# A planned retention-and-MLP kernel: scaled values issued behind their masks, a smaller lead of attention, and a new order of the first loads

## The chip, the cores and the metric

The kernel runs on one core of one Trainium2 chip. The metric is the device time of one execution in microseconds (us). Shares and durations come from one profiled execution of the kernel before; its instructions are named by their line in the kernel, as L442. PE is TensorE (matmuls), PEld its weight loads, DVE is VectorE, ACT is ScalarE, POOL is GpSimd and SP is SyncE. POOL issues the loads of this kernel; SP issues its stores and the DMA transposes.

## What is computed

Retention (attention with a decay in place of a softmax) over 8 batches, 8 heads, 576 positions and 64 dimensions a head, and behind it an MLP with an exact GELU on the 4608 tokens:

```python
scores = scale * np.matmul(q, k.transpose(0, 1, 3, 2))
Dmat = np.where(rel >= 0, gamma[:, None, None] ** rel[None, :, :], 0.0)
attn = np.matmul(scores * Dmat[None], v)                 # 8 x 8 x 576 x 64
x = attn.transpose(0, 2, 1, 3).reshape(4608, 512)
h = x @ w_in                                             # 512 -> 2048
g = 0.5 * h * (1.0 + erf(h / sqrt(2)))
out = g @ w_out                                          # 2048 -> 512, float32
```

All inputs are float32 in memory. The kernel turns them to bf16 in the loading DMA.

## The kernel before

**Units.** The work of attention is cut into 36 units of 128 tokens. Units 0 to 3 are the first 128 positions of batches 0 to 3. Then come, for each pair of batches, two units for each further 128 positions (4 and 5, 6 and 7, 8 and 9 for the first pair) and one unit that holds the last 64 positions of both batches (10 for the first pair; 11 and 12 are positions 128 to 255 of the second pair, 17 is its tail, and so on). A unit whose positions are the first 128 of its batch is called raw: it uses v as it is loaded. For every other unit v is first multiplied by a decay on DVE, `scaled_v`, L334 to L341, which writes the tile vh.

**Steps of a unit.** T: q and k are turned, for units 0 to 7 on PE (`turn`, L285, tile qk_ps, copied to qkT), from unit 8 on by a DMA transpose that SP issues (`turn_dma`, L298). A: 8 matmuls make the scores (`scores`, L307), and two DVE multiplications mask them (`masked`, L318, tile ret). B: 8 matmuls with v or vh (`inner`, L343, tile o_ps). U: the running state of a pair of batches takes in k and vh (`state`, L360, tile u_ps). X: 4 matmuls with that state (`cross`, L393), and one multiplication or copy that writes the unit's 128 columns of xT (`evacuate`, L407).

**Blocks.** The MLP runs in 9 blocks of 512 tokens, that is of 4 units: `mlp1` (L437) multiplies xT by w_in, 64 matmuls of 512 columns a block, with a GELU on ACT; `mlp2` (L460) multiplies by w_out, 64 matmuls a block, then ACT copies and SP stores. Blocks 0 and 1 have their mlp1 cut into two halves of 256 tokens (L496), so that it can begin with two units; from block 2 on it needs all four units of its block.

**Who sets the order.** The file is a planner. While it writes the program it keeps a model of the time of each engine (`T`), of the landing of each load (`sw_dma`, L169) and of each DMA transpose (`turn_dma`), and at each step it issues what its model says is ready. Only the order of instructions on each engine comes from it. On the chip each engine takes its instructions in that order and waits at each for its inputs, whatever the model thought.

**Loads.** POOL issues them in the order of a list written out by hand, `ORDER` (L223): `q1` is q of unit 1, `wi3` the fourth eighth of w_in, `wo0` the first eighth of w_out, `io` the constants on POOL, `dq2` a POOL multiplication for a decay table. When a pair's state has taken in its k and vh, the loads of a later unit (11 and up) are put behind the list (`reload`, L389). q and k of unit 0 come by two DMAs of SP and ACT (L97).

**Lead of attention.** In blocks before the last, step A is allowed in places between the matmuls of mlp2, and only while the number of units begun is at most four times the block's number plus `AHEAD` (L616). Together with A of a group (a pair, or a tail) the planner issues B and X of the groups before it, when their masks are done.

**When v is scaled.** `fire` (L535) issues `scaled_v` for units in a fixed order as soon as the model says that v has landed (L551 to L556), up to six units before the states that use them.

**Warm-up.** Six matmuls on zeros (L570) run before the first data; in later gaps before 16 us of planned time the planner fills with more of them (L673).

Of the kernel before, what the change touches and what calls it, by code (L numbers as in the profile page):

```python
# [17 lines left out]
def kernel(  # L18
# [24 lines left out]
    N_DF = d_ff // 128  # L43
# [18 lines left out]
    kept = pair_of[1, 0]  # L62
# [6 lines left out]
    N_LD = 9  # L69
    N_QKT = 8  # L70
    N_VH = 6
    AHEAD = 11

    const = ctx.enter_context(tc.tile_pool(name="const", bufs=1))
    ld_pool = ctx.enter_context(tc.tile_pool(name="ld", bufs=N_LD))
# [84 lines left out]


    sw = [0.0]
    flying = []
    dq_done = {1}
    land = {}
# [3 lines left out]
    def sw_dma(issue, move):  # L169
        if len(flying) >= 8:  # L170
            T["pool"] = max(T["pool"], flying[-8])
        at = T["pool"]
        T["pool"] += issue
        sw[0] = max(sw[0] + move, at + 4.95 + move - 0.9)
        flying.append(sw[0])
        return sw[0]

# [7 lines left out]
    def load(what, i):  # L185
# [30 lines left out]
        else:  # L216
# [3 lines left out]
    tiles_of(0)  # L220
    land["q", 0], land["k", 0] = 4.5, 4.6
    cast_due = {("q", 0): (loaded[0][0][:, 0], first["q32"]), ("k", 0): (loaded[0][0][:, 1], first["k32"])}
    ORDER = ("q1 k1 wi0 io v1 q2 k2 q3 k3 v0 v3 wi1 v2 wi2 k4 wi3 wi4 wi5 wi6 q4 v4 wo0 k5 wi7 q5 wo1 wo2 wo3 v5 k6 q6 "  # L223
             "wo4 q7 v8 k7 dq2 wo5 wo6 q8 wo7 v7 dq3 dq4 v6 q9 k10 k9 v9 k8 q10 v10").split()

    def next_order():
        item = ORDER.pop(0)
# [38 lines left out]
    def pe(dur, to="full"):  # L266
        if mode[0] != to:
            T["pe"] += 0.11
            mode[0] = to
        T["pe"] += dur  # L270
        return T["pe"] + DRAIN


# [11 lines left out]
    def turn(i, jj):  # L285
        s = st[i]
        qk = loaded[i][0]
        if "qkT" not in s:
            s["qkT"] = tr_pool.tile([128, 2, HP, 128], BF16, tag="qkT", name="qkT")
        b, t = bank([128, HP, 128], BF16, "qk_ps")  # L290
        for hp in range(HP):
            nc.tensor.transpose(t[:, hp, :], qk[:, jj, 2 * hp:2 * hp + 2, :], ident1)  # L292
        done = pe(0.3 if T["pe"] < 9 else 0.225)
        done = either(0.42, done, s["qkT"][:, jj], t)
        release(b, done + 0.05)
        s["T", jj] = done + SEM

    def turn_dma(i):  # L298
        s = st[i]
        s["qkT"] = tr_pool.tile([128, 2, HP, 128], BF16, tag="qkT", name="qkT")  # L300
        nc.sync.dma_start(s["qkT"].rearrange("p j hp s -> p (j hp) s"),
                          loaded[i][0].rearrange("p j h d -> p (j h d)"), transpose=True)
        at = on("sp", 1.3, land["k", i])
        sw[0] = max(sw[0] + 1.8, at)
        s["T", 0] = s["T", 1] = at + 8.0

    def scores(i):  # L307
        s = st[i]
# [151 lines left out]
    def mlp2(t, ts, m0, m1):  # L460
        cols = slice(ts * 128, ts * 128 + 128)
        if (t, ts) == (N_BLK - 1, 2):
            if m1 < N_DF:
                return
            for lo, hi in ((0, 256), (256, 384), (384, 512)):
                b, oT = bank([128, d_model], FP32, "oT")
                for m in range(N_DF):
                    nc.tensor.matmul(oT[:, :hi - lo], lhsT=g_tiles[t, m // 2][:, m % 2, cols],  # L468
                                     rhs=w_out_sb[m // 2][:, m % 2, lo:hi], start=(m == 0), stop=(m == N_DF - 1))
                done = pe(N_DF * ((hi - lo) / 2400 + 0.0025))  # L470
                o_sb = o_pool.tile([128, hi - lo], FP32, tag=f"o_sb{lo}", name="o_sb", bufs=1)
                nc.scalar.copy(o_sb, oT[:, :hi - lo])
                release(b, on("act", 0.17 + (hi - lo) * 0.00084, done))
                for row, p0, n in rows_of(t, ts):
                    nc.sync.dma_start(out[row:row + n, lo:hi], o_sb[p0:p0 + n])
            return
        if m0 == 0:
            acc[t, ts] = bank([128, d_model], FP32, "oT")
        b, oT = acc[t, ts]
        for m in range(m0, m1):  # L480
            nc.tensor.matmul(oT, lhsT=g_tiles[t, m // 2][:, m % 2, cols], rhs=w_out_sb[m // 2][:, m % 2, :],  # L481
                             start=(m == 0), stop=(m == N_DF - 1))
        done = pe((m1 - m0) * 0.2158)
        if m1 == N_DF:
            o_sb = o_pool.tile([128, d_model], FP32, tag="o_sb", name="o_sb")
            nc.scalar.copy(o_sb, oT)  # L486
            release(b, on("act", 0.6, done) + SEM)
            for row, p0, n in rows_of(t, ts):
                nc.sync.dma_start(out[row:row + n, :], o_sb[p0:p0 + n])

    def x_ready(t, lo, hi):
        return max(x_at.get(i, 1e9) for i in range((t * TOK + lo) // C, (t * TOK + hi - 1) // C + 1))

    runs = []
    for t in range(N_BLK):
        if t < 2:  # L496
            for lo in (0, 256):
                runs.append([("1", t, m, 2, lo, lo + 256) for m in range(0, N_DF, 2)])
        else:
            runs.append([("1", t, m, 1, 0, TOK) for m in range(N_DF)])  # L500
        order = range(4) if t < N_BLK - 1 else (3, 0, 1, 2)
        if t == 0:
            runs.append([("2", t, ts, m, m + 2) for m in range(0, N_DF, 2) for ts in range(2)])
            runs.append([("2", t, ts, m, m + 4) for ts in range(2, 4) for m in range(0, N_DF, 4)])
        else:
            runs.append([("2", t, ts, m, m + 4) for ts in order for m in range(0, N_DF, 4)])
# [28 lines left out]
    def fire():  # L535
# [14 lines left out]
            on(engine, dur, now)  # L550
        while nV < N_U and nV < len(s_done) + N_VH and ("v", v_order[nV]) in land:  # L551
            i = v_order[nV]
            if land["v", i] + 0.1 > now or i in kept and i + 4 > nB or nA < 4 and T["dve"] > now:
                break
            scaled_v(i)
            nV += 1  # L556
# [10 lines left out]
        release(b, T["pe"])  # L567

    T["pe"] = 1.3
    for _ in range(6):  # L570
        b, t = bank([128, 512], FP32, "warm")
        nc.tensor.matmul(t, lhsT=zeros[:, :128], rhs=zeros, start=True, stop=True)
        release(b, 0.0)
    T["pe"] = 4.9
    while True:
# [28 lines left out]
        if nA < N_U:  # L604
# [3 lines left out]
            if all(("T", 1) in st[i] and ("T", 0) in st[i] for i in g):  # L608
                ready = max(max(st[i]["T", 0], st[i]["T", 1]) for i in g)
                back = [i for i in range(nB, nA) if st[i]["R"] <= now and (i in raw or "V" in st[i])]  # L610
                n = 2 * len(g) + len(back)
                ok = nA - nB <= 2
                if early or stuck:
                    cand(max(ready, free_time(2)) if ok else 1e9, "A", g, [])
                elif head is None or head[1] == 0 or head[0] == "2" and 4 <= head[3] <= 8 and head[1] < N_BLK - 1:
                    if len(back) == nA - nB and (head is None or nA + len(g) <= 4 * head[1] + AHEAD):  # L616
                        cand(max(ready, free_time(min(n, 8 - len(held))) - 0.3), "A", g, back)
        if nT < N_PE_TR and nT <= nA + 3:
            key = ("qk"[half], nT)
# [50 lines left out]
        if not waits:  # L670
            break
        gap = min(waits) - now
        if now < 16 and gap > 0.35:  # L673
            warm(max(1, int(gap / 0.2158 * (0.5 if now < 9 else 0.8))))
        T["pe"] = max(T["pe"], min(waits))
    assert nX == N_U and not any(runs), (nA, nB, nX, nT, nV, [len(r) for r in runs])

# [29 lines left out]
```

## Time and profile before

| What | Value |
|---|---|
| Median of 3 runs | 310.3 us (307.86 to 312.0) |
| The profiled execution | 309.51 us, of which the span of its instructions is 307.7 us |
| PE, PEld, busy | 296.8 us (96%), 158.9 us (52%) |
| ACT, POOL, DVE, busy | 136.0 us, 114.0 us, 97.1 us |
| L442 (mlp1) and L481 (mlp2) on PE | 127.3 us in 704, 126.5 us in 560 |
| L329 (masks) on DVE | 35.7 us in 56 and 10.2 us in 16 |
| L339 (vh) on DVE | 23.4 us in 36, 682 ns each |
| Granted TensorE clock | 1.00 in each of the stretches of 10 us up to 130 us |

The profile shows one execution on the core. Its timeline gives, for each engine, the start, the duration, the line and the tiles of groups of instructions, and in brackets how long the engine was idle before and what ended the wait. A view of the waits sums these by pair of instructions. The chain of work that ended last follows the span back from its end, at each step to what released it. The landing of each DMA is known from the semaphore that it updates.

### The profile page before, as it was taken

What the parts mean: (1) busy time and instruction counts of PE and PEld (TensorE: products, weight loads), DVE (VectorE), ACT (ScalarE), POOL (GpSimd) and SP (SyncE); (2) the same over time, 40 slices, a digit from 0 to 9 for tenths busy, and PEclk for the clock granted to TensorE, in tenths of its full rate; (3) what the DMA queues carried; (4) which work ended last, traced back from release to release, by engine and by line L of the source; (5) the groups of instructions that cost most, each with busy time, mean ns of one, the idle gap of its engine ahead of it and who ended that gap; (6) DMA issues with size and microseconds to landing.
All of it is one profiled execution on the core that took longest, in us unless ns stands there. A gap on an engine that the chain in (4) does not pass through costs nothing.

```text
span 307.7 us, 5630 instructions
## 1 busy us (share of the span) xinstructions
PE 296.8 (96%) x2354; PEld 158.9 (52%) x2354; DVE 97.1 (32%) x185; ACT 136.0 (44%) x237; POOL 114.0 (37%) x143
## 2 busy tenths in 40 slices
PE   7999999989959999999999999999999999999996
PEld 2488575855424554445445554454446444544445
DVE  6851446334543181018001851073006300400000
ACT  5286154633316622653266226631663166216611
POOL 8987899942348474105311863100000000000000
PEclk9999999999999999999999999999999999999999
DMA  9999999999999999965990999923000110010022
GB/s 142 162 191 183 177 181 214 169 151 136 169 191 186 138 156 174 194 56 86 150 159 2 167 166 174 148 69 104 34 0 36 51 54 0 36 68 34 2 60 76
DMA packets 154042, 35.76 MB, mean 116 GB/s; under 512 B 143009, under 2 KB 149537, under 8 KB 154017
## 3 DMA queue, kind: packets, MB, share of 16 engines
q0 software_dynamic: 116832, 18.10, 83.3%
q1 hardware_dynamic: 36144, 17.05, 28.8%
q8 instruction: 18, 0.29, 0.4%
q10 hardware_dynamic: 1040, 0.26, 0.4%
q14 instruction: 8, 0.06, 0.1%
HBM read 36.70 MB, written 9.44 MB: 150 GB/s over the span
## 4 chain that ended last, share of the span: by engine, by line
PE 70%; DMA 17%; POOL 10%; issue 2%; DVE 0%; ACT 0%; POOLq 0%; DVEq 0%
PE hT L442 31%; PE oT L481 30%; DMA v_ld<-in_v_dram 6%; DMA qk_ld<-in_q_dram 4%; POOL qk_ld L217 4%; DMA w_in<-in_moe_w_in_dram 3%; DMA w_out<-in_moe_w_out_dram 3%; POOL v_ld L217 3%; PE o_ps L351 2%; PE sc L314 2%; DMA qk_ld<-in_k_dram 2%; PE o_ps L403 2%; POOL w_in L191 1%; PE oT L468 1%; POOL dqT L199 1%
## 5 line engine op out<-in xcount | busy, mean ns | idle before, releaser
L442 PE MATMUL hT<-xT,w_in 128*128 128x512 bf16 (+1 forms) x704 | 127.3, 340 | 3.4 <-DVE xT L423 3.2
L481 PE MATMUL oT<-w_out,g 128*128 128x512 bf16 x560 | 126.5, 379 | 0.0
L448 ACT ACTIVATE g<-hT 128x512 bf16<-128x512 f32 x144 | 85.6, 597 | 42.3 <-PE hT L442 42.2
L442 PEld LDWEIGHTS <-w_in 128*128 128x128 bf16 x704 | 68.6, 98 | 60.4 <-issue 3.5
L481 PEld LDWEIGHTS <-g 128*128 128x128 bf16 x560 | 53.5, 98 | 60.4
L329 DVE TENSOR_TENSOR ret<-sc,msk 128x512 bf16<-128x512 f32 x56 | 35.7, 683 | 99.8 <-PE sc L314 99.8
L486 ACT COPY o_sb<-oT 128x512 f32<-128x512 f32 x35 | 20.4, 586 | 89.6 <-PE oT L481 73.0
L217 POOL DMA_DIRECT2D qk_ld<-in_q_dram x31 | 27.8, 898 | 47.0 <-PE u_ps L369 31.5
L217 POOL DMA_DIRECT2D v_ld<-in_v_dram x32 | 28.9, 906 | 8.0 <-DMA qk_ld<-in_q_dram 5.6
L282 ACT CAST u_sb<-u_ps 64x512 bf16<-64x512 f32 x31 | 18.0, 580 | 25.6 <-PE u_ps L369 24.4
L217 POOL DMA_DIRECT2D qk_ld<-in_k_dram x31 | 27.9, 900 | 3.7 <-DMA v_ld<-in_v_dram 2.9
L339 DVE TENSOR_TENSOR vh<-v_ld,dv 128x512 bf16<-128x512 bf16 x36 | 23.4, 682 | 12.4 <-DMA v_ld<-in_v_dram 12.4
L329 DVE TENSOR_TENSOR ret<-sc,near 128x512 bf16<-128x512 f32 x16 | 10.2, 682 | 35.9 <-PE sc L314 35.9
L423 DVE TENSOR_TENSOR xT<-o_ps,dqT 128x512 bf16<-128x512 f32 x28 | 18.1, 682 | 5.7 <-PE o_ps L403 5.7
L314 PE MATMUL sc<-qkT 64*128 64x128 bf16 x288 | 12.8, 223 | 2.4 <-DMA qkT<-qk_ld 2.4
L314 PEld LDWEIGHTS <-qkT 64*128 64x128 bf16 x288 | 8.3, 96 | 6.1 <-DMA qkT<-qk_ld 2.9
L351 PEld LDWEIGHTS <-vh 128*64 128x64 bf16 x224 | 6.7, 109 | 6.8 <-issue 5.9
L280 DVE COPY qkT<-qk_ps 128x512 bf16<-128x512 bf16 x13 | 5.3, 421 | 13.0 <-PE qk_ps L292 12.9
L351 PE MATMUL o_ps<-ret,vh 128*64 128x128 bf16 x224 | 9.3, 222 | 0.0
L403 PE MATMUL o_ps<-qkT,u_sb 128*128 128x128 bf16 (+1 forms) x128 | 9.1, 214 | 0.0
L213 POOL DMA_DIRECT2D v_ld<-in_v_dram x8 | 5.4, 680 | 9.4 <-DMA v_ld<-in_v_dram 3.9
L213 POOL DMA_DIRECT2D qk_ld<-in_q_dram x8 | 5.6, 706 | 4.7 <-DMA v_ld<-in_v_dram 2.2
(51 smaller groups left out, 94.1 us busy)
## 6 DMA issues: line engine op xcount, KB each, us to landing
out_dram<-o_sb SPq DMA_DIRECT2D x31, 256.0 KB, 4.6
v_ld<-in_v_dram POOLq DMA_DIRECT2D x32, 128.0 KB, 8.4
qk_ld<-in_q_dram POOLq DMA_DIRECT2D x31, 128.0 KB, 8.3
qk_ld<-in_k_dram POOLq DMA_DIRECT2D x31, 128.0 KB, 8.1
w_in<-in_moe_w_in_dram POOLq DMA_DIRECT2D x8, 256.0 KB, 7.0
w_out<-in_moe_w_out_dram POOLq DMA_DIRECT2D x8, 256.0 KB, 8.3
out_dram<-o_sb SPq DMA_DIRECT2D x9, 128.0 KB, 3.5
qk_ld<-in_k_dram POOLq DMA_DIRECT2D x8, 64.0 KB, 12.1
```

Of the source, the lines that this page charges most:

```text
L217: nc.gpsimd.dma_start(dst, src[2 * bp + j, :, ci * C:ci * C + C, :].rearrange("h s d -> s h d"))
L282: nc.scalar.copy(dst, src)
L314: nc.tensor.matmul(got[e][1][:, hp, :], lhsT=qkT[sl, 1, hp, :], rhs=qkT[sl, 0, hp, :], start=True, stop=True)
L329: nc.vector.tensor_tensor(r, t, by, op=ALU.mult)
L339: nc.vector.tensor_tensor(vh, loaded[i][1], dv[:, :, ci:ci + 1].to_broadcast([128, H, D]), op=ALU.mult)
L351: nc.tensor.matmul(o[64 * e:64 * e + 64, hp, :], lhsT=vals[:, 2 * hp + e, :], rhs=s["ret"][e][:, hp, :], start=(hp == 0), stop=(ci == 0 an ...
L403: nc.tensor.matmul(o[:, hp, cols], lhsT=u[:, jj, hp, :], rhs=s["qkT"][:, 0, hp, cols], start=False, stop=(hp == HP - 1), skip_group_check= ...
L423: nc.vector.tensor_tensor(dst, o, by, op=ALU.mult)
L442: nc.tensor.matmul(hT[:, m, :], lhsT=w[:, cc, o:o + 128], rhs=xT[:, cc, t * TOK + lo:t * TOK + hi], start=(cc == 0), stop=(cc == N_DM - 1))
L448: nc.scalar.activation(g_tiles[t, m0 // 2][:, m0 % 2:m0 % 2 + n, lo:hi], hT, AF.Gelu)
L481: nc.tensor.matmul(oT, lhsT=g_tiles[t, m // 2][:, m % 2, cols], rhs=w_out_sb[m // 2][:, m % 2, :], start=(m == 0), stop=(m == N_DF - 1))
L486: nc.scalar.copy(o_sb, oT)
```

## The change

Six things are changed, all in the planner:

1. **vh behind its masks.** `scaled_v` of a unit is issued only when step A of that unit has been issued (`nA <= i` ends the loop). For the two kept units (2 and 3, whose loads stay in place) it waits until eight units are begun, and for a raw unit until DVE is free in the model.
2. **Lead.** `AHEAD` goes from 11 to 9, with 2 added again from block 2 on: only blocks 0 and 1 have another limit, 9 and 13 units in place of 11 and 15.
3. **Model of transfers.** A load's latency is 5.3 in place of 4.95; transposes are taken one after the other, 3.1 each, and each takes 2.2 of the load queue's time; a store takes 0.7 of it. A transpose is planned for when q and k have both landed.
4. **Load order.** `ORDER` is written anew: wi0 and v0 come sooner, q1 later, k8 eleven places sooner, v3 later, and the weights w_in are spread.
5. **Cuts.** mlp1 of block 0 is cut into 256, 128 and 128 tokens in place of 256 and 256.
6. **Warm-up.** Eight matmuls on zeros in place of six; the model takes a matmul before 7.5 us as twice as long; gaps over 0.2 us are filled in full.

```diff
-    AHEAD = 11
+    AHEAD = 9
+    HOT = 7.5
...
+    turned = [0.0]
...
-        sw[0] = max(sw[0] + move, at + 4.95 + move - 0.9)
+        sw[0] = max(sw[0] + move, at + 5.3 + move - 0.9)
...
-    ORDER = ("q1 k1 wi0 io v1 q2 k2 q3 k3 v0 v3 wi1 v2 wi2 k4 wi3 wi4 wi5 wi6 q4 v4 wo0 k5 wi7 q5 wo1 wo2 wo3 v5 k6 q6 "
-             "wo4 q7 v8 k7 dq2 wo5 wo6 q8 wo7 v7 dq3 dq4 v6 q9 k10 k9 v9 k8 q10 v10").split()
+    ORDER = ("k1 wi0 io q1 v0 q2 k2 v1 wi1 k3 v2 q3 wi2 wi3 wi4 v3 q4 wi5 k4 q5 k5 wi6 wo0 wo1 wi7 v4 wo2 v5 wo3 "
+             "q6 k6 k7 dq2 q7 wo4 q8 k8 wo5 wo6 v6 v7 wo7 dq3 q9 k9 v8 dq4 v9 q10 k10 v10").split()
...
-        T["pe"] += dur
+        T["pe"] += dur * (2.0 if T["pe"] < HOT else 1.0)
...
-        done = pe(0.3 if T["pe"] < 9 else 0.225)
+        done = pe(0.225)
...
-        at = on("sp", 1.3, land["k", i])
-        sw[0] = max(sw[0] + 1.8, at)
-        s["T", 0] = s["T", 1] = at + 8.0
+        at = on("sp", 1.3, max(land["q", i], land["k", i]))
+        turned[0] = max(turned[0], at) + 3.1
+        sw[0] = max(sw[0], at) + 2.2
+        s["T", 0] = s["T", 1] = turned[0] + 3.4
...
                 nc.sync.dma_start(out[row:row + n, :], o_sb[p0:p0 + n])
+            sw[0] += 0.7
...
-            for lo in (0, 256):
-                runs.append([("1", t, m, 2, lo, lo + 256) for m in range(0, N_DF, 2)])
+            cuts = (0, 256, 384, 512) if t == 0 else (0, 256, 512)
+            for lo, hi in zip(cuts, cuts[1:]):
+                runs.append([("1", t, m, 2, lo, hi) for m in range(0, N_DF, 2)])
...
-            if land["v", i] + 0.1 > now or i in kept and i + 4 > nB or nA < 4 and T["dve"] > now:
+            if land["v", i] + 0.1 > now or nA <= i or i in kept and nA < 8 or i in raw and T["dve"] > now:
                 break
...
-    for _ in range(6):
+    for _ in range(8):
...
-                    if len(back) == nA - nB and (head is None or nA + len(g) <= 4 * head[1] + AHEAD):
+                    if len(back) == nA - nB and (head is None or nA + len(g) <= 4 * head[1] + AHEAD + 2 * (head[1] > 1)):
...
-        if now < 16 and gap > 0.35:
-            warm(max(1, int(gap / 0.2158 * (0.5 if now < 9 else 0.8))))
+        if now < 16 and gap > 0.2:
+            warm(max(1, round(gap / (0.43 if now < HOT else 0.23))))
```

## The prediction, made before the result was known

> **What bounds the kernel now.** I read the page first, then PE's waits, then PE's timeline from end to start, then the queues of DVE, POOL and SP where PE waited.
>
> ```profile
> span 307.7 us, 5630 instructions
> PE 296.8 (96%) x2354; PEld 158.9 (52%) x2354; DVE 97.1 (32%) x185; ACT 136.0 (44%) x237; POOL 114.0 (37%) x143
> ...
> DMA  9999999999999999965990999923000110010022
> ```
>
> PE is the bound, but 96% also counts warm-up matmuls. The DMA row is full up to about 130 us: before that an order can only choose what lands first.
>
> ```profile
> PE hT L442 <- DVE xT L423: 3.2, 1, 3.2
> PE sc L314 <- DMA qkT<-qk_ld: 2.4, 3, 1.3
> ```
>
> These two are nearly all that PE waits for behind the start: 5.6 us, in four places.
>
> ```profile
> 9.52 1.30 PE L565 MATMUL warm<-zeros 128*128 128x512 bf16 x3
> ...
> 14.35 0.64 PE L351 MATMUL o_ps<-ret,v_ld 128*64 128x128 bf16 x16 [0.27 <-DMA v_ld<-in_v_dram]
> ...
> 15.69 1.91 PE L442 MATMUL hT<-xT,w_in 128*128 128x256 bf16 x16
> ...
> 67.22 0.40 PE L314 MATMUL sc<-qkT 64*128 64x128 bf16 x8 [1.29 <-DMA qkT<-qk_ld]
> ...
> 77.50 0.40 PE L314 MATMUL sc<-qkT 64*128 64x128 bf16 x8 [0.25 <-DMA qkT<-qk_ld]
> ...
> 85.07 0.40 PE L314 MATMUL sc<-qkT 64*128 64x128 bf16 x8 [0.81 <-DMA qkT<-qk_ld]
> ...
> 90.52 13.97 PE L442 MATMUL hT<-xT,w_in 128*128 128x512 bf16 x64 [3.22 <-DVE xT L423]
> ```
>
> In PE's timeline the MLP begins at 15.69, once v0 has landed (14.30). No idle time is noted from 19.57 to 65.9, nor from 90.52 to the end of the matmuls at 305. So what can be won lies before 19.57 and in the stretch from 65 to 91.
>
> ```profile
> 80.29 1.28 DVE L339 TENSOR_TENSOR vh<-v_ld,dv 128x512 bf16<-128x512 bf16 x2
> 89.18 0.69 DVE L339 TENSOR_TENSOR vh<-v_ld,dv 128x512 bf16<-128x512 bf16 x1 [7.61 <-DMA v_ld<-in_v_dram]
> 89.78 1.28 DVE L423 TENSOR_TENSOR xT<-o_ps,dqT 128x512 bf16<-128x512 f32 x2
> ```
>
> DVE stood 7.61 us at one vh. Counting vh along the planner's order, it is unit 16's, whose v is not used before block 3. Behind it in DVE's queue were the two xT of units 11 and 12, whose matmuls had ended at 82.9; block 2 needs unit 11. That is the 3.22 us.
>
> ```profile
> 72.07 17.08 DMA v_ld<-in_v_dram
> ```
>
> The chain of waits has that load: issued at 72.07, landed 17.08 us later.
>
> ```profile
> 47.91 6.45 SPq L489 DMA_DIRECT2D out_dram<-o_sb  x4
> 54.54 20.03 SPq L301 DMA_TRANSPOSE qkT<-qk_ld  x6
> ```
>
> SP issued the first transpose (unit 8) at 54.54, behind the four stores of block 0 and behind k8, landed at 51.61. The transposes of units 8 to 12 landed at 64.0, 67.2, 71.5, 74.4 and 77.5, one each 3.4 us, and steps A of 9 and 12 waited for theirs.
>
> **The change, part by part.** *vh behind masks.* No instruction goes or comes: 36 vh of 0.68 us stay, they move on DVE. vh16 now stands behind A of 16, in block 2, so it can't hold the xT of unit 11: -3.2 us. Late next in that place: nothing within 3 us, as xT of 11 and 12 would end at 82.9 + 1.3 = 84.2, and mlp2 covers PE until 87.3. What it adds: B of a unit waits for masks and then vh. In block 2 DVE already has that pattern (masks end at 110.22, two vh until 111.42) and B begins at 111.53; the second vh is used 0.28 later. The cover is 0.1 to 0.4 us: cost 0. If it goes, each group pays up to 1.3 us, for about 14 groups.
>
> *Lead.* A of 13 and 14 (83.86 to 85.4) leaves block 1, with the 0.81 wait in it. It runs in block 2 at the same 0.55 us: 0. Block 2 then has three groups (13 and 14; 15 and 16; 17) for its four places; unit 15, which block 3 needs, stands in the second.
>
> *Model and order, transposes.* I laid the new order out by the trace's own steps: 0.88 us of POOL an issue (0.75 for weights), 8 loads in flight, 4.95 us to landing, then 0.86 us a unit load and 1.31 a weight. On the old order this gives 14.2 for v0 (trace 14.30) and 54.4 for v10 (55.06). On the new one k8 lands at 41.8 in place of 51.6. Unit 8's transpose then stands before block 0's stores on SP. Eight transposes, 18 unit loads and four stores landed between 55 and 90. With 0.86 a load and 0.5 to 1.3 a store (two landed 0.48 apart; a weight load of its size takes 1.31) this leaves (35 - 15.5 - 2.0 to 5.2) / 8 = 1.8 to 2.2 us of queue a transpose, so each of 8 and 9 puts what is behind it back by 2. With up to 10.8 us to land (the longest row): 8 by 53, 9 by 63, 10 by 67, 11 by 71, 12 by 75. Their places in mlp2 of block 1, with the waits gone, are 64.7 for 8 and 9, 68.7 for 10, 74.0 for 11 and 12. So 1.29 and 0.81 go and unit 12 stays tight. For it I take the 0.25 of the 77.50 row. Ends: 0 and 2.4 us. Sum: -2.35 + 0.25 = -2.1.
>
> The cost is that w_out 5 to 7 and v6, v7 land 2 us later, at about 45 to 49.5. PE then has the first half of block 1's mlp1 (36.7 on, 7.0 us) and wo4 to wo6: 0, and if that cover is gone, up to 2 us. The trace prices the crowding: v of 16 needed 17.08 us among transposes, loads near 30 us 8.4. The Trainium skill, "DMA: Bandwidth & Descriptors", section "Issuing engines are not separate DMA queues", speaks against the early transpose: queues of different engines share the same 16 DMA engines and interleave. By it alone nothing is gained in transfer, and the sum would keep the 2.35.
>
> *Start.* v0 lands at 9.4 and v1, now the last needed for the first half, at 12.3 (old: v0 at 14.30). B of 1, its xT (0.7), and mlp1 can begin at 13.75: 1.9 us sooner. But w_in now paces PE: wi1 13.6, wi2 17.6, wi3 18.9, wi4 20.2, wi5 23.2, wi6 27.1 (old 24.3), wi7 31.0 (old 29.5), and v3 comes at 21.0 (old 14.8). Each eighth brings 1.77 us of mlp1 (8 x 0.109 + 16 x 0.056). Filling in the rest (T of 2 to 5 at 0.22 a half, B at 0.28, A at 0.28), PE has all of block 0's mlp1, A of 4 and 5 and four mlp2 matmuls done at 32.9; the trace of before has the same at 33.34. So -0.4. Ends: -1.4 (no idle) and +1.0 (each landing half a microsecond worse). *Cuts.* 128 matmuls of 128 columns for 64 of 256: 128 x 0.056 - 64 x 0.109 = +0.2, in the 1.77 already; 16 GELUs of 256 for 8 of 512 add about 1.4 us on ACT, which was busy 7.1 of 10 us there: 0, else 1.4.
>
> *Warm-up.* The six stand 0.64 apart; eight and one filler end at 7.0 in place of 5.64, so T of unit 0 begins up to 1.3 later. A of 0 moves from 7.9 to at most 9.2, its masks to 10.6, those of unit 1 to 11.9, still before v1: 0, at worst 1.3. HOT says 7.5; the matmul pitch fell from 0.43 to 0.22 only between 10.35 and 10.88. The skill's "TensorE: Matmul & The Clock Gate", section "What's actually happening", puts the step behind one free-running window of about 3.4 us of sustained work, not behind a count. By it the eight would bring the step to near 5 to 8; here that would shorten only work that ends before v1 lands, again 0.
>
> *Sum* against the profiled execution: 309.5 - 3.2 - 2.1 - 0.4 + 0.1 for semaphores between the changed steps (bounds 0 and 0.4, the cover above) = 303.9. Its own time is 0.8 below the median of 310.3; against that it is 2.1% less.
>
> **The rivals.** *The start keeps all it wins:* 1.9 us, if wi and v3 land in time for PE never to idle. For it: PE noted nearly no wait for weights before (PEld 0.3). Against: wi6 and v3 come later than before. 309.5 - 5.3 - 1.9 = 302.3.
>
> *Transposes stay late:* the DMA row was full in any order, so the 2.35 merely moves to later units, and the start gives nothing: 309.5 - 3.2 = 306.3. Against: k8 is 10 us sooner.
>
> *Slower: the last group of block 1 misses its place.* With the limit of 13 units, 11 and 12 are the last, and block 2 needs unit 11. If transpose 12 lands after the third place (74.0) and the fourth (about 78.3, 4.3 us later, as 71.1 to 76.3 in the trace), A, masks, vh, B and X stand bare: 0.55 + 4 x 0.61 + 1.2 + 1.1 + 1.3 = 6.6 us, in place of the 5.3 saved: 309.5 - 5.3 + 6.6 = 310.8. If unit 15 does the same in block 3, 317. For it: 12 landed at 77.5 before, 0.8 from that point. Against: it now has a queue start of 10 us, and few loads ahead.
>
> *It does nothing to the DVE wait* can hardly be: no order is left in which vh16 precedes xT of 11, as 15 and up aren't begun in block 1.
>
> **How the numbers follow.** Forecast 0.48 (303.9, its own range 302.8 to 305.4, from -1.4 on the start and up to +1.5 on transpose 12), start in full 0.19 (301.0 to 302.8), transposes late 0.17 (305.4 to 307.5), slower 0.16 (308 to 317). The range 301.0 to 309.0 leaves out the lower tail of the second (0.05) and most of the slower case (0.12). Two per cent, about what a measurement of this kernel can tell from no change, is 304.1 and 316.5. Faster: half of the forecast's share, all of the second's, and some for runs before that lay above the profiled one: 0.48. Slower by 2%: only the repeated miss and what I don't see, 0.10. The rest 0.42.
>
> **What would show it.** On DVE no vh before the masks of its own unit and no gap of several us on v between 80 and 90: step one right. PE's wait at the first 512-wide L442 gone; if it stays but names DMA or masks, the slower rival. SP's first transpose before its first store of out, near 42; landings of 8 to 12 before 75. First L442 near 13.75, and idle or warm matmuls between 15 and 24 where wi or v3 is late. From block 2 on PE without idle; waits of L351 for vh there would mean that the cover of 0.1 to 0.4 was too thin. If the span lies below 299, something at the start was worth more than the 1.9 I can see.

## The result, and the profile after

| What | Before | Changed |
|---|---|---|
| Median | 310.17 us (307.67 to 312.0, 15 runs) | 307.31 us (306.76 to 307.93, 15 runs) |
| The profiled execution, its span | 309.51, 307.7 us | 307.32, 305.6 us |
| Ratio of the times, 95% interval | | 0.9917 [0.9889, 0.9945] |

The changed kernel is faster, by 0.8%. Against the profiled execution before, the forecast took off 5.6 us; 2.2 came. Of the 2.9 us between the medians a part goes, by before's executions beside the experiments, with a lower granted TensorE clock in two of three of them (see the last section). The line numbers shift: L442 is now L445 (mlp1), L481 L484 (mlp2), L314 L317 (scores), L339 L342 (vh), L351 L354 (B), L369 L372 (states), L403 L406 (X), L423 L426 (xT), L301 L303 (DMA transposes), L282 L284 (the copy of a state).

From the page of the changed kernel, the lines that answer to the first ones shown of before:

```profile
span 305.6 us, 5759 instructions
...
PE 296.2 (97%) x2391; PEld 160.3 (52%) x2425; DVE 99.7 (33%) x187; ACT 135.7 (44%) x243; POOL 113.8 (37%) x143
...
DMA  9999999999999999995918999992000210010022
```

PE's busy time has hardly changed, and the DMA row is full as far as before. What PE waits for has changed; the view of its waits, changed kernel (total us, times, longest):

```profile
PE u_ps L372 <- ACT u_sb L284: 2.5, 2, 1.3
PE warm L577 <- DVE zeros L100: 1.2, 1, 1.2
...
PE hT L445 <- DVE xT L426: 0.2, 1, 0.2
```

Both rows of before that the forecast went after are gone: 3.2 us of mlp1 for xT is 0.2, and the 2.4 us of the scores for DMA transposes has no row left. (The warm-up row is the first microsecond, as in before.) A row that was not there stands on top: a state (L372) waits twice for a copy on ACT. PE's timeline of the changed kernel shows where:

```profile
14.48 1.91 PE L445 MATMUL hT<-xT,w_in 128*128 128x256 bf16 x16
...
64.73 1.03 PE L484 MATMUL oT<-w_out,g 128*128 128x512 bf16 x3
...
136.08 0.64 PE L354 MATMUL o_ps<-ret,v_ld 128*64 128x128 bf16 x16
136.65 0.62 PE L317 MATMUL sc<-qkT 64*128 64x128 bf16 x16
...
161.48 0.64 PE L354 MATMUL o_ps<-ret,vh 128*64 128x128 bf16 x16
161.95 0.42 PE L372 MATMUL u_ps<-vh,qk_ld 128*64 128x64 bf16 x16
163.64 0.44 PE L372 MATMUL u_ps<-vh,qk_ld 128*64 128x64 bf16 x16 [1.27 <-ACT u_sb L284]
...
228.62 0.44 PE L372 MATMUL u_ps<-vh,qk_ld 128*64 128x64 bf16 x16 [1.28 <-ACT u_sb L284]
```

Read the rows from 136.08 on. B of the raw pair 18 and 19 (it uses v_ld, not vh) is followed by scores, not by the pair's state. The state comes 25 us later, at 161.95, and the next state of the same batches is the next thing on PE, at 163.64, after 1.27 us of idle PE. Both add into the same tile u_ps, and the second has to wait until the first one's sum has been copied out (two copies on ACT, 1.18 us from 162.41 on). In before the state stood right behind its own B:

```profile
141.23 0.64 PE L351 MATMUL o_ps<-ret,v_ld 128*64 128x128 bf16 x16
141.70 0.42 PE L369 MATMUL u_ps<-vh,qk_ld 128*64 128x64 bf16 x16
```

Why the state was put off stands in DVE's queue of the changed kernel:

```profile
135.17 0.68 DVE L342 TENSOR_TENSOR vh<-v_ld,dv 128x512 bf16<-128x512 bf16 x1
137.08 2.48 DVE L332 TENSOR_TENSOR ret<-sc,msk 128x512 bf16<-128x512 f32 x4 [1.23 <-PE sc L317]
139.48 1.89 DVE L342 TENSOR_TENSOR vh<-v_ld,dv 128x512 bf16<-128x512 bf16 x3
```

One vh (unit 18) stands at 135.17. The second raw unit's, 19, comes only in the three behind the masks of the next group. It is the clause `i in raw and T["dve"] > now` (`i in raw`: the unit is a raw one; `T["dve"] > now`: the model has DVE busy): when the planner came to vh of 19, its model had DVE still busy with vh of 18, so it put 19 off, and by the next time the masks of 20 and 21 were in the queue. A state is issued only when both of its vh exist, so it missed its place. The same happened to the next pair of batches, at 228.62.

The start of mlp1 of each block (the first 512-wide row of L442 or L445 in PE's timeline) shows how the time goes and comes:

| Block | 2 | 3 | 4 | 5 | 6 | 7 | 8 |
|---|---|---|---|---|---|---|---|
| Before | 90.52 | 121.77 | 152.11 | 185.28 | 215.62 | 247.10 | 277.11 |
| Changed | 84.59 | 116.62 | 146.71 | 181.60 | 211.69 | 244.88 | 274.89 |
| Ahead | 5.93 | 5.15 | 5.40 | 3.68 | 3.93 | 2.22 | 2.22 |

At block 2 the changed kernel was 5.9 us ahead. Block 2 took 0.78 longer than before; the scores of unit 14 (0.33), which in before stood in block 1, are now in it. Each pair of blocks with a late state lost 1.72 and 1.71 and won 0.25 in the block that the state had left: -1.47 and -1.46. With 0.1 in the tail: 5.93 - 0.78 - 1.47 - 1.46 - 0.1 = 2.1, the difference of the spans.

### The profile page after: what moved, and what is told of

Same layout as the page of the kernel before. It is cut to its first block, busy times and chain, and to the rows that moved or that the text cites. A ratio compares the mean times of both kernels' runs of the same rounds, so it can differ in the third digit from the quotient of the medians.

```text
span 305.6 us, 5759 instructions
## 1 busy us (share of the span) xinstructions
PE 296.2 (97%) x2391; PEld 160.3 (52%) x2425; DVE 99.7 (33%) x187; ACT 135.7 (44%) x243; POOL 113.8 (37%) x143
## 5 line engine op out<-in xcount | busy, mean ns | idle before, releaser
L445 PE MATMUL hT<-xT,w_in 128*128 128x512 bf16 (+2 forms) x758 | 127.9, 325 | 0.8 <-DVE xT L426 0.2
L484 PE MATMUL oT<-w_out,g 128*128 128x512 bf16 x538 | 123.5, 379 | 1.2 <-issue 0.2
L451 ACT ACTIVATE g<-hT 128x512 bf16<-128x512 f32 (+1 forms) x152 | 86.9, 574 | 48.1 <-PE hT L445 47.6
L445 PEld LDWEIGHTS <-w_in 128*128 128x128 bf16 x768 | 69.6, 98 | 56.8 <-DVE xT L426 0.4
L484 PEld LDWEIGHTS <-g 128*128 128x128 bf16 x560 | 53.4, 98 | 60.2
L219 POOL DMA_DIRECT2D qk_ld<-in_q_dram x31 | 27.9, 901 | 42.2 <-DMA qkT<-qk_ld 15.8
L342 DVE TENSOR_TENSOR vh<-v_ld,dv 128x512 bf16<-128x512 bf16 x36 | 23.4, 684 | 1.9 <-DMA v_ld<-in_v_dram 1.9
L284 ACT CAST u_sb<-u_ps 64x512 bf16<-64x512 f32 x26 | 15.1, 579 | 15.5 <-PE u_ps L372 15.2
L426 DVE TENSOR_TENSOR xT<-o_ps,dqT 128x512 bf16<-128x512 f32 x28 | 18.2, 683 | 10.8 <-PE o_ps L406 10.8
L282 DVE CAST u_sb<-u_ps 64x512 bf16<-64x512 f32 x6 | 4.1, 688 | 45.7 <-PE u_ps L372 45.6
L317 PE MATMUL sc<-qkT 64*128 64x128 bf16 x288 | 12.3, 220 | 0.0
L354 PEld LDWEIGHTS <-vh 128*64 128x64 bf16 x224 | 6.8, 109 | 7.4 <-issue 5.9
L317 PEld LDWEIGHTS <-qkT 64*128 64x128 bf16 x288 | 8.2, 95 | 3.2 <-issue 1.1
L354 PE MATMUL o_ps<-ret,vh 128*64 128x128 bf16 x224 | 9.7, 223 | 0.0
L372 PE MATMUL u_ps<-vh,qk_ld 128*64 128x64 bf16 x256 | 6.8, 196 | 2.8 <-ACT u_sb L284 2.5
L406 PE MATMUL o_ps<-qkT,u_sb 128*128 128x128 bf16 (+1 forms) x128 | 9.3, 214 | 0.0
```

The source lines that it names most:

```text
L219: nc.gpsimd.dma_start(dst, src[2 * bp + j, :, ci * C:ci * C + C, :].rearrange("h s d -> s h d"))
L284: nc.scalar.copy(dst, src)
L317: nc.tensor.matmul(got[e][1][:, hp, :], lhsT=qkT[sl, 1, hp, :], rhs=qkT[sl, 0, hp, :], start=True, stop=True)
L342: nc.vector.tensor_tensor(vh, loaded[i][1], dv[:, :, ci:ci + 1].to_broadcast([128, H, D]), op=ALU.mult)
L354: nc.tensor.matmul(o[64 * e:64 * e + 64, hp, :], lhsT=vals[:, 2 * hp + e, :], rhs=s["ret"][e][:, hp, :], start=(hp == 0), stop=(ci == 0 an ...
L406: nc.tensor.matmul(o[:, hp, cols], lhsT=u[:, jj, hp, :], rhs=s["qkT"][:, 0, hp, cols], start=False, stop=(hp == HP - 1), skip_group_check= ...
```

## The experiments

The theory was: the two double states cost 2.9 us, from the clause for raw units alone, and without it the forecast's middle stands. The rivals were that the time went at the start (order of loads, warm-up), that it went in block 2 (13 and 14 taken apart), or that the five edits beside the vh rule bring something that the masks rule (no vh of a unit before its step A, `nA <= i`) does not.

e1, e2, e4 and e5 ran in one sitting, on one chip, e6 to e12 in two others on a second chip. Before's median was 310.30 in the first, 309.51 beside e6 to e9 and 309.23 beside e10 to e12, so a difference of less than about a microsecond between runs of different sittings can't be told from none. What the profiles show is one execution of each.

**e1, the changed kernel without the clause for raw units** (before's clause for the first four units in its place).

```diff
-            if land["v", i] + 0.1 > now or nA <= i or i in kept and nA < 8 or i in raw and T["dve"] > now:
+            if land["v", i] + 0.1 > now or nA <= i or i in kept and nA < 8 or nA < 4 and T["dve"] > now:
```

> The changed kernel, with the wait of a raw unit's vh for an idle DVE kept only for the first four units. Theory: the changed kernel won 5.9 us up to block 2 and gave 2.9 back in blocks 4 and 6, where the state of a raw pair (18 and 19, 27 and 28) is issued in one go with the state of the next pair and has to wait for the first copy out of u_ps (1.27 and 1.28 us named, 1.4 with the matmuls' tail, plus mode changes). The state then stands behind its own pair again: span 305.6 - 2.9 = 302.7, ratio to before 0.982, no wait of L372 for ACT. Rival: the wait is ACT's or DVE's own load and moves elsewhere: span 305 or more, ratio 0.990.

Measured: 304.54 us (304.24 to 304.93), ratio to before 0.982 [0.9791, 0.985], span 302.7. PE's timeline of e1:

```profile
136.24 0.64 PE L354 MATMUL o_ps<-ret,v_ld 128*64 128x128 bf16 x16
136.71 0.42 PE L372 MATMUL u_ps<-vh,qk_ld 128*64 128x64 bf16 x16
...
161.89 0.64 PE L354 MATMUL o_ps<-ret,vh 128*64 128x128 bf16 x16
162.36 0.42 PE L372 MATMUL u_ps<-vh,qk_ld 128*64 128x64 bf16 x16
162.71 0.62 PE L317 MATMUL sc<-qkT 64*128 64x128 bf16 x16
```

The state stands behind its own B again, and the next one goes without a wait. Up to there the order of PE's instructions is that of the changed kernel; mlp1 of blocks 2 and 3 begins within 0.2 us of it (84.75, 116.78), block 8 at 272.12 in place of 274.89. The clause costs 2.8 us: 307.31 against 304.54, both far from the other's spread. The theory holds.

**e2, the kernel before with the masks rule alone.**

```diff
-            if land["v", i] + 0.1 > now or i in kept and i + 4 > nB or nA < 4 and T["dve"] > now:
+            if land["v", i] + 0.1 > now or nA <= i or i in kept and i + 4 > nB or nA < 4 and T["dve"] > now:
```

> The kernel before with one condition added: no vh of a unit that is not begun. Theory: DVE's 7.6 us wait for v of unit 16 and PE's 3.2 behind it go, and A of 13 and 14 leaves block 1 with its 0.8 of waiting; the 1.29 and 0.25 on transposes stay. Span 307.7 - 3.2 - 0.8 = 303.7, ratio 0.987. Rival: the transfers are full in any order, so that PE waits for something else in the same place: span 306 to 308, ratio 0.995 to 1.0.

Measured: 304.51 us (303.62 to 305.39), ratio 0.9825 [0.9791, 0.9859], span 301.9. Of PE's waits in e2 one row of the two shown of before is left, and it is small:

```profile
PE sc L314 <- DMA qkT<-qk_ld: 0.4, 1, 0.4
```

One more condition, `nA <= i`, gives as much as the whole change without its clause. That was more than expected: the wait for xT went, as it should, and 2.0 of the 2.4 us for transposes went too, with the old order of loads. Of these, 0.8 were expected to go, as the scores of 13 and 14 leave block 1; the other 1.2 were not. The transposes of units 9 to 12 landed at 65.97, 68.79, 72.24 and 75.60, 1.2 to 2.7 us sooner than in before. Why is not settled: with the same rule, and with POOL's loads in the same order, e10 below has them where before had them (67.64 to 77.57), and the profiled execution of e2 is the fastest of its six. So the wait for transposes can go without the new order, but this one execution does not show that it always does.

**e4, the clause for raw units alone, on the kernel before.**

```diff
-            if land["v", i] + 0.1 > now or i in kept and i + 4 > nB or nA < 4 and T["dve"] > now:
+            if land["v", i] + 0.1 > now or i in kept and i + 4 > nB or (nA < 4 or i in raw) and T["dve"] > now:
```

> The kernel before, with only the wait of every raw unit's vh for an idle DVE. Theory: the double state needs both edits, since without the masks rule raw vh are issued long before their states: no two states in a row, ratio 1.00 (0.995 to 1.005), if anything less, as one vh no longer stands where it blocked DVE. Rival: the clause alone costs the 2.9 us: ratio 1.009.

Measured: 309.06 us (307.31 to 311.7, 12 runs), ratio 0.9969 [0.9937, 1.0001]; PE's waits have no row of L369. Where vh runs up to six units ahead of its states, putting one off costs nothing that these runs can tell. The clause needs the masks rule to hurt.

**e10, both conditions on the kernel before.**

```diff
-            if land["v", i] + 0.1 > now or nA <= i or i in kept and i + 4 > nB or nA < 4 and T["dve"] > now:
+            if land["v", i] + 0.1 > now or nA <= i or i in kept and i + 4 > nB or (nA < 4 or i in raw) and T["dve"] > now:
```

(The line taken out is that of the kernel before, as in e2 and e4.)

> The kernel before with the masks rule and with the wait of every raw unit's vh for an idle DVE, nothing else. Theory: only together do the two make the double states, in the order of PE three times (blocks 1, 4 and 6), each at 1.45 us, and 11 to 14 are split as well (0.4 to 0.8): 304.5 of the masks rule alone + 4.4 + 0.6 = 309.5, ratio 0.997 or more; L372 waits for the copy out of u_ps three times. Rival: the double states cost only with the new load order and model: ratio 0.983 as with the masks rule alone.

Measured: 316.71 us (316.16 to 317.0), ratio 1.0234 [1.02, 1.0269], span 315.0: slower than before, and 12.2 us slower than e2. The interaction is as expected, its size is not. Three states are doubled, and the first one stands in block 1, where nothing covers it; PE's timeline of e10:

```profile
84.33 0.64 PE L351 MATMUL o_ps<-ret,vh 128*64 128x128 bf16 x16
84.80 0.42 PE L369 MATMUL u_ps<-vh,qk_ld 128*64 128x64 bf16 x16
86.49 0.44 PE L369 MATMUL u_ps<-vh,qk_ld 128*64 128x64 bf16 x16 [1.28 <-ACT u_sb L282]
...
87.42 0.62 PE L403 MATMUL o_ps<-qkT,u_sb 128*128 128x128 bf16 x8
...
89.21 0.43 PE L314 MATMUL sc<-qkT 64*128 64x128 bf16 x7 [0.73 <-DVE ret L329]
92.80 0.59 PE L442 MATMUL hT<-xT,w_in 128*128 128x512 bf16 x1 [3.16 <-DVE xT L423]
```

All of block 1's mlp2 is done by 84.33. The double state, X of units 11 and 12 and the scores of the next units then stand bare, and on DVE the xT of 11 and 12 begins only at 92.06, behind two copies of together 1.39 us, the masks of two units and two vh. mlp1 of block 2 starts at 92.80 against e2's 83.95, 8.85 us later, of which 0.9 were there at mlp2 of block 1 (65.14 and 64.28). Block 2 then takes 1.4 us more than e2's, and the two later doubles bring 1.5 each: 13.2, against 13.1 between the spans.

**e5, e1 with units 13 and 14 taken together** (the model's time to land for a transpose made 1 us shorter).

```diff
-        s["T", 0] = s["T", 1] = turned[0] + 3.4
+        s["T", 0] = s["T", 1] = turned[0] + 2.4
```

> The first kernel of this call, and the transposes planned 1.0 us earlier, so that A of 11 and 12 takes the place one mlp2 step (0.86 us) sooner, B of 11 and 12 stands before the last mlp2 matmuls of block 1, and 13 and 14 are not split over blocks 1 and 2. Theory: block 2's 0.8 us longer time and the 0.2 wait before it go: span 301.8, ratio 0.979. Rival: the transpose of 12 has not landed when A of it comes, and PE waits there for up to 2 us: ratio 0.982 or worse.

Measured: 304.21 us (303.54 to 304.8), ratio 0.9811 [0.978, 0.9841], span 302.3. Block 2 takes 31.91 us against e1's 32.03, and PE waits for nothing at all behind the start. Against e1 that is 0.3 us in the median, which these runs can't tell from none. Before's block 2 takes 31.25, but without the scores of 13 and 14 (0.55 us together), which e5 and e2 (31.91 too) have in it: block 2 is not where the time went. It is the fastest median seen, level with e1 and e2, and it is the base of e6 to e9.

**e6, e5 with the old warm-up.**

```diff
-        T["pe"] += dur * (2.0 if T["pe"] < HOT else 1.0)
+        T["pe"] += dur
...
-        done = pe(0.225)
+        done = pe(0.3 if T["pe"] < 9 else 0.225)
...
-    for _ in range(8):
+    for _ in range(6):
...
-        if now < 16 and gap > 0.2:
-            warm(max(1, round(gap / (0.43 if now < HOT else 0.23))))
+        if now < 16 and gap > 0.35:
+            warm(max(1, int(gap / 0.2158 * (0.5 if now < 9 else 0.8))))
```

> The kernel with no split (302.3), with the warm-up of before: six first matmuls, gaps filled as before, no doubled durations. Theory: in the changed kernel PE is never idle from 1.2 to 17 us, since more matmuls on zeros were planned than the gaps hold, and T, A and B of the first units queue behind them: first L445 at 14.5 to 15.1 where loads alone allow 13.75. With fewer, first L445 near 14.0 and span 0.7 less, 301.6, ratio 0.979. Rival (my prediction): the warm-up lies beside the landing of v1 and costs nothing: 302.3, first L445 unchanged.

Measured: 305.05 us (303.88 to 307.41, 12 runs), ratio 0.9903 [0.9863, 0.9942]. The program has 15 warm-up matmuls before the first of mlp1 in place of 24. mlp1 begins at 13.42 (e5: 15.06), mlp2 of block 1 at 64.15 (e5: 65.31). The gain of 1.2 us was expected to stay and did not; PE's timeline of e6:

```profile
75.06 0.40 PE L317 MATMUL sc<-qkT 64*128 64x128 bf16 x8
77.28 0.40 PE L317 MATMUL sc<-qkT 64*128 64x128 bf16 x8 [1.82 <-DMA qkT<-qk_ld]
```

The scores of unit 12 wait 1.82 us for its transpose, which was issued at 68.72 once k12 had landed at 68.58; in the changed kernel it was issued at 65.46. So the sooner start ran into the next limit, the landing of unit 12. The runs lie in two clusters, seven at 303.9 to 305.2 and five at 306.7 to 307.4. All five of the upper one had a mean granted clock of 0.994, six of the lower seven 1.00; the trace shows one of the lower, so what took the clock down is open.

**e7, e5 with the old load order** (the `ORDER` lines of the diff taken back).

> The kernel with no split, with the load order of before. Theory: since w_in and v3 pace PE up to 33 us, the new order is worth little at the start (0.3 us or less), and later it only saves transpose waits of 0.4 to 1.5 us: span 302.5 to 304, ratio 0.982 to 0.987. Rival: the new order is worth all of the 1.9 us of its earlier first L445 and the transposes besides: span 304.5 or more, ratio 0.988 or more.

Measured: 305.05 us (304.59 to 305.93), ratio 0.988 [0.9846, 0.9915]. mlp1 begins at 16.90, and the scores of unit 9 wait 1.38 us for a transpose at 68.33. In this surrounding the new order is worth 0.8 us in the median, near the least that these runs can tell, and it is not the order alone: with the old one the planner writes 31 warm-up matmuls before the first of mlp1, in place of 24.

**e12, e2 with the new load order and nothing else.**

```diff
-    ORDER = ("q1 k1 wi0 io v1 q2 k2 q3 k3 v0 v3 wi1 v2 wi2 k4 wi3 wi4 wi5 wi6 q4 v4 wo0 k5 wi7 q5 wo1 wo2 wo3 v5 k6 q6 "
-             "wo4 q7 v8 k7 dq2 wo5 wo6 q8 wo7 v7 dq3 dq4 v6 q9 k10 k9 v9 k8 q10 v10").split()
+    ORDER = ("k1 wi0 io q1 v0 q2 k2 v1 wi1 k3 v2 q3 wi2 wi3 wi4 v3 q4 wi5 k4 q5 k5 wi6 wo0 wo1 wi7 v4 wo2 v5 wo3 "
+             "q6 k6 k7 dq2 q7 wo4 q8 k8 wo5 wo6 v6 v7 wo7 dq3 q9 k9 v8 dq4 v9 q10 k10 v10").split()
```

> The kernel before with the masks rule and the new load order, its warm-up, cuts, model and lead as before. Theory: first L445 near 13.5 to 14 as in the kernel with the old warm-up, 1.5 us sooner than with the masks rule alone; w_in, v3 and the halves of mlp1 give back at least 1 of it, and transposes decide the rest: 303 to 305.5, no clear difference from the masks rule alone (304.5). Rival: order is worth its 1.5 to 1.9 us at the end: 302.8 or less.

Measured: 307.0 us (306.46 to 309.28, 12 runs), ratio 0.9938 [0.9905, 0.9972]: 2.5 us slower than e2, which was not expected. PE's timeline of e12:

```profile
13.51 1.91 PE L442 MATMUL hT<-xT,w_in 128*128 128x256 bf16 x16
...
17.33 1.05 PE L442 MATMUL hT<-xT,w_in 128*128 128x256 bf16 x8 [0.67 <-DMA w_in<-in_moe_w_in_dram]
...
19.60 1.92 PE L442 MATMUL hT<-xT,w_in 128*128 128x256 bf16 x16 [0.90 <-DMA w_in<-in_moe_w_in_dram]
...
85.29 0.40 PE L314 MATMUL sc<-qkT 64*128 64x128 bf16 x8 [2.17 <-DMA qkT<-qk_ld]
```

mlp1 begins at 13.51, but twice waits for w_in, and at 85.29 the old model takes up a unit whose transpose is not there yet. (Mlp1 of block 2 begins at 87.80, in e2 at 83.95.) e1 and e5 have the new order and are level with e2, so the other edits win that back; which of them does is not shown.

**e8, e5 with the old cuts.**

```diff
-            cuts = (0, 256, 384, 512) if t == 0 else (0, 256, 512)
+            cuts = (0, 256, 512)
```

> The kernel with no split, with mlp1 of block 0 in halves again. Theory: the second half then waits for unit 3 (v3 lands at 21), PE idles about 0.8 us more before 23 us and saves 0.2 of matmuls of 128 columns: span 302.9, ratio 0.983. Rival: the cut is only overhead, ACT's eight more GELUs included: span 302.0, ratio 0.980.

Measured: 304.98 us (304.75 to 305.59), ratio 0.9879 [0.9846, 0.9912]. PE waits 0.5 us for xT at 23.18 and 0.5 for qkT at 19.80, where the cut kernel has work. The cuts are worth about 0.8 us in the median with the new order, again near the least that can be told.

**e9, e5 with six warm-up matmuls and none after 6 us of planned time.**

```diff
-    for _ in range(8):
+    for _ in range(6):
...
-        if now < 16 and gap > 0.2:
+        if now < 6 and gap > 0.2:
```

> The kernel with no split, with six first matmuls and no filling of gaps behind 6 us of planned time. Theory of the queue: nothing stands ahead of T, A and B, first L445 at 13.8 to 14.0, span 301.3, ratio 0.978. Rival, the clock: without the fill the pitch stays at half rate beyond the first L445 (a pitch of 0.43 for 512 columns up to 15 us or later), each microsecond of it costs half a microsecond, and the span is 303 or more, ratio 0.983 or more.

Measured: 304.71 us (303.62 to 307.3), ratio 0.9875 [0.9829, 0.9921]. mlp1 of block 0 in e9, PE's timeline:

```profile
14.46 3.57 PE L445 MATMUL hT<-xT,w_in 128*128 128x256 bf16 x16
```

It begins 0.6 us sooner than in e5, but its 16 matmuls take 3.57 us in place of 1.91, and PE runs at the full pitch only from 18.7. The filling costs PE's time before mlp1 and gives it back in mlp1's pitch: 304.71 against 304.21 can hardly be told apart.

**e11, e1 with the old warm-up** (the edit of e6, on e1).

> The first kernel of the study (raw wait for four units only, A of 11 and 12 in the later place), with the warm-up of before. Theory: the start's gain of 1.0 to 1.6 us at the first L445 was given back in the no-split kernel because PE came to A of 12 before its transpose (1.82); one mlp2 step later it waits less than 1 us or not at all: median 303.7, few runs above 306. Rival: the transposes themselves come late whenever PE is early, whatever the place: the same spread from 304 to 307.4, median 305.

Measured: 304.99 us (304.54 to 308.06), ratio 0.9875 [0.9827, 0.9922]. The profiled execution has no wait for a transpose, as expected with units 11 and 12 taken later, but it began mlp1 at 15.45: the full pitch came only at 15.0, and v1 landed at 12.91 (e6: 12.03). So this run neither shows nor refutes that the sooner start of e6 can be kept. Its one run at 308.06 had a granted clock of 0.994, the other five 1.00.

## Why the prediction was right in part, and where it failed

The sum forecast 303.9 and 307.3 came. The difference is one term that was not in the sum (+2.9) and one that had the wrong size (the start, +0.16 in place of -0.4). That 307.3 lies where the rival with late transposes had put its share (305.4 to 307.5) is luck: the transposes were not late.

**vh behind masks, the wait removed: right.** -3.2 was forecast; 3.22 became 0.23, so -3.0. The xT of 11 and 12 runs right behind its matmuls, as the prediction laid out; DVE's queue of the changed kernel:

```profile
79.92 1.28 DVE L342 TENSOR_TENSOR vh<-v_ld,dv 128x512 bf16<-128x512 bf16 x2
83.84 1.29 DVE L426 TENSOR_TENSOR xT<-o_ps,dqT 128x512 bf16<-128x512 f32 x2 [2.63 <-PE o_ps L406]
```

No gap on v is left between 80 and 90. Two short ones (0.39 and 1.47) are at 31.86 and 34.02, and no wait of PE follows from them.

**What the vh rule adds: this is the step that failed.** The prediction costed the waiting vh at 0, by following one pattern, masks and then two vh in front of B, and it said what each group would pay if the cover went. That part nearly held: only B of 15 and 16 waits, 0.2 us (its row at 108.76 lasts 0.85 in place of 0.64, as the two vh end at 109.13). But B is not the only reader of vh. States read it too, and a raw unit's vh has no other reader. The wait of a raw unit's vh for an idle DVE was listed in the change and costed nowhere: a term put at nothing without a reason. The trace of before had the row to ask at: at 141.23 and 141.70 the state of a raw pair stands directly behind its B, so anything that put one of its two vh off by one step moved the state out of its place. What was late next was another state on the same tile, with a copy between them: 2.93 us by the block starts, 2.5 of them idle PE, and 2.8 by the experiment that takes only the clause out. None of the rivals held this case. The slower rival had steps of 11 and 12 standing bare before block 2; that did appear, in e10, but there the double state stood first, and unit 12's transpose had landed at 77.57.

**Transposes: right in size, but not by its reason alone.** -2.1 was forecast; the three waits of 2.35 are gone and no 0.25 came for unit 12. k8 stands twelve places sooner in the list (not eleven) and landed at 41.65 (forecast 41.8), SP issued unit 8's transpose at 41.74, and units 8 to 12 landed at 50.15, 60.62, 67.07, 71.27 and 74.06 (forecast: by 53, 63, 67, 71, 75). Two of its readings were off without changing that. Between 55 and 90 us 19 unit loads landed and not 18, which takes 0.1 off its queue time of a transpose. And its places for the scores, 64.7, 68.7 and 74.0, were early: before's rows less their waits give 65.5, 70.6 and 75.6, and the changed kernel had them at 65.69, 70.62 and 76.75, so unit 12 was less tight than it said. (The distance of 71.1 to 76.3 that it gives as 4.3 is 5.2.) On the weighing with the Trainium skill, "DMA: Bandwidth & Descriptors", section "Issuing engines are not separate DMA queues": taken alone its sentence would have kept the 2.35, and the chip kept none of it. But the order has no sole claim to the gain. With the masks rule and the old order, PE waits for transposes 0.4 us in e2, and unit 9 alone 1.19 in e10 and 1.38 in e7: so between 1.0 and 2.0 of the 2.35 went without the new order, and it differs from one execution to the next.

**Lead: right that it costs nothing, wrong that it does something.** Units 13 and 14 were to leave block 1. Unit 13 stayed (its scores are at 83.96) and 14 moved to 99.72, and this comes from the model of transposes, as e5 shows, where 1 us less in that model takes both together (at 99.20). The lead has no part in it: e2, with the old lead, has both at 98.73, and with only the lead of the changed kernel put back the planner writes the same instructions in the same order on every engine.

**Start: the term that was mis-sized.** -0.4 was forecast; at mlp2 of block 1 the changed kernel stands at 64.73, before at 64.57: +0.16. The landings were right (v0 9.75, v1 12.29, wi5 to wi7 at 23.20, 27.10 and 30.98, v3 21.04; none is off by more than 0.4), and yet mlp1 began at 14.48, not 13.75, and PE never waited for w_in. What was wrong was the price of the warm-up, "0, at worst 1.3", because it was followed only as far as the eight and their first filler. It put the masks of unit 1 at 11.9, before v1; they ended at 12.91, after it. PE's and DVE's timelines of the changed kernel:

```profile
9.10 0.94 PE L570 MATMUL warm<-zeros 128*128 128x512 bf16 x3
9.87 0.61 PE L294 MATMUL qk_ps<-ident,qk_ld 128*128 128x128 bf16 x8
...
11.19 0.40 PE L317 MATMUL sc<-qkT 64*128 64x128 bf16 x8
...
13.15 0.41 PE L354 MATMUL o_ps<-ret,v_ld 128*64 128x128 bf16 x8
13.50 0.40 PE L317 MATMUL sc<-qkT 64*128 64x128 bf16 x8
13.83 0.82 PE L570 MATMUL warm<-zeros 128*128 128x512 bf16 x3
```

```profile
11.62 1.29 DVE L332 TENSOR_TENSOR ret<-sc,near 128x512 bf16<-128x512 f32 x2 [0.19 <-PE sc L317]
```

q1 had landed at 8.38, but the turning of unit 1 (9.87) stands behind three fillers, and so its scores, its masks and its B (13.15) come late. The xT of unit 1 ended at 14.19, and three more fillers keep mlp1 until 14.48.

By e6 the -0.4 was right for the order of loads and the warm-up cost 0.6: with the old warm-up mlp1 begins at 13.42 and mlp2 of block 1 at 64.15, which is -0.42 against before. But e11, with the same start, has mlp2 of block 1 at 65.39; its full pitch came some 6 us later and its first loads landed 0.9 later (q1 at 9.59 and v1 at 12.91; e6: 8.68 and 12.03). And the three executions with the new warm-up (changed, e1, e5) have it at 64.73, 64.89 and 65.31. So it is shown that mlp1's beginning was bounded here by PE's own queue, warm-up in it, and not by w_in; how much of the 0.56 the warm-up costs stays open, as the start differs by more than that between executions. That e6's time is no better is, in its profiled execution, the next limit, unit 12's transpose, which the prediction had named as the tight one.

**The other edits together.** e1 has all of them, e2 none, and they are level (304.54 and 304.51). Taken one by one from e5, order and cuts are each worth about 0.8 us in the median, no more than the sittings differ by, and the order put on e2 alone costs 2.5. Together they bring no time that these runs can tell.

**What beats both kernels.** e1, e2 and e5, at 304.2 to 304.5, are 2.8 to 3.1 us faster than the changed kernel. e2 does it with one condition.

## What to carry to other kernels

When an edit delays a step, list every reader of what the step writes, and for each the place in the queue that it must not miss; a step put off by less than a microsecond can move its reader by a whole round of the schedule. Two accumulations into one tile with a copy of it between them should not be neighbours on PE (1.27 us of idle PE here). Where a change consists of several conditions, cost each one by itself, the smallest too: here one clause took back half of what another one gave.

## What the runs showed of the hardware that was not expected

**The step to the full matmul pitch is not fixed by the program.** The changed kernel, e1 and e5 have the same order of instructions on PE up to 60 us, and their first matmuls at the full pitch (0.22 us for 512 columns, 0.056 for 128) come at 9.4, 9.8 and 10.6 us; the first of mlp1 follows at 14.48, 14.64 and 15.06. With less filling it came at 15.0 in e11 and 18.7 in e9. The granted clock of the profile is 1.00 in each of the stretches between 5 and 21 us in e9 and e11 all the same, so here the pitch of the matmuls has to be read, not the clock row. The Trainium skill, "TensorE: Matmul & The Clock Gate", section "What's actually happening", has a free-running window with about half a microsecond of spread either way; the three runs of one order, 1.2 us from first to last, come near that. e6 and e11 have the same program up to unit 11 and reached the pitch some 6 us apart (8 transposing matmuls took 0.62 us in e6 at 8.73 and 1.04 in e11 at 9.63): that is more than the half microsecond, and PE's short idle times before 10 us, which differ between the two, are only a possible reason.

**What a stall costs beside its length.** In before PE idled 3.22 us ahead of mlp1 of block 2 and then ran it at full pitch (13.81 us from its first matmul to the next block of mlp2, granted clock 1.00). In e10 the idle time there was 3.16, but PE had been busy for only 3.62 of the 9 us from 84 to 93; the granted clock was lower in these and in the 7 us behind them (stretch, its length, PE's busy time, granted clock, DMA share, GB/s):

```profile
84.00:93.00 9.00, 3.62 (x83) 0.80 1.73 189
93.00:100.00 7.00, 6.78 (x25) 0.77 2.10 189
```

Mlp1 of block 2 took 15.49 us there. So of two stalls of one length, the one amid other gaps cost 1.7 us more.

**The granted clock of whole executions.** Of before's 51 executions in the three sittings 17 had a mean granted clock of 0.999 or more and took 308.2 us on average; 34 had 0.995 or less and took 310.5. The changed kernel had 0.999 or more in all 15 of its executions, e1, e2 and e5 in all 18 of theirs; e10 had 0.989 to 0.994 in all six. A clock lower by 0.006 over 308 us is 1.8 us, as an estimate, and the two groups of before are 2.3 apart. So against before's executions at 0.999 or more the changed kernel's median is 0.9 us ahead, not 2.9, and e1 and e2 are 3.7 ahead. Where before loses the clock is not shown, since its profiled execution had 1.00 (at 309.51 it is among the longest of the first group, 306.7 to 309.6); the gaps ahead of block 2, where e10 loses it, are gone from the changed kernel.
